# A hand-written order for the start of an attention + MoE kernel, and weights' lower parts without GpSimd

## The chip, the cores and the metric

The kernel runs on one core of a Trainium2 chip. The metric is the device time of one execution in microseconds (us). A core has five engines that matter here: TensorE (PE; PEld is its weight load) multiplies matrices, VectorE (DVE) and ScalarE (ACT) do elementwise work, GpSimd (POOL) does elementwise work and issues DMAs, and SyncE (SP) issues DMAs. Each engine takes its instructions in the order in which the compiler queued them. Matrix products go to PSUM; all other tiles lie in SBUF.

## The reference

```python
# q, k, v: [8, 8, 576, 64];  w_in: [512, 2048];  w_out: [2048, 512]; drawn inputs scale q by 8.0 and k by 4.405
q_s = softmax(q, axis=-1)              # over the 64 of a head
k_s = softmax(k, axis=2)               # over the 576 of the sequence
kv  = einsum('bhsd,bhse->bhde', k_s, v)
x   = einsum('bhsd,bhde->bhse', q_s, kv)      # then heads side by side: [4608, 512]
h   = x @ w_in
out = (h * clip(h + 3, 0, 6) / 6) @ w_out     # [4608, 512], float32
```

(The softmaxes add 1e-9 to their sums.)

## The kernel before, in words

The 4608 tokens are nine blocks of 512. The hidden width 2048 is 16 chunks `f` of 128. For a block `j` and a chunk `f`, `gemm1` makes 128 hidden rows (12 matmuls of 128x512 into a PSUM tile `ph`), applies the activation (ScalarE L567, VectorE L568) and splits the result `g` into an upper part `g_hi` (ScalarE, L123) and a lower part `g_lo` (VectorE, L124). `gemm2` adds that chunk's share to the four PSUM tiles `po` of the block (12 matmuls). Each product is made from upper and lower parts of both factors: hi*hi, hi*lo and lo*hi. Blocks 0 and 1 run in this form; blocks 2 to 8 take two chunks at a time by a scheme of seven products (`fast_pair`), whose combined weights block 1 works out (`fast_weights`) and stores to DRAM.

The weights arrive as raw 64-bit numbers, 1 MB a chunk (`load_w`, SyncE's queue). `decode(f)` turns them into 32-bit floats: ScalarE takes the magnitude (L145) and scales the low words (L156); VectorE clamps (L146), shifts (L148), merges the sign (L153) and adds the low words (L157); then `split` copies the upper part on ScalarE (L123) and subtracts on L124 for the lower part. That last subtraction is GpSimd's for odd chunks from 3 on, and VectorE's for the others. The tile `m` of a decode has one buffer, `v` two.

Attention of a block is done for four head pairs `hp`: the k softmax (VectorE km L262, ScalarE Exp L263, transposes on TensorE, copies L271 and L272), the q softmax (block 0: VectorE qm L252, GpSimd L253, ScalarE Exp L254, VectorE qr L255 to L257, GpSimd L258; transposes; copy L359), the product `pkv` with its normalisation into `kv` (VectorE L210 to L213), then `px` and its split into `x_hi` (ScalarE) and `x_lo` (VectorE). For block 0 the operands lie in the buffers of the weight chunks 15 to 8, which are loaded later. From block 2 on the softmax of q takes other lines (L292 to L302) and uses GpSimd for small copies (`swap` L284, `kb` L335).

What sets the order: the framework's scheduler simulates the program at compile time and orders each engine's instructions by readiness and by the order in which the program wrote them. `keep_in_program_order` fixes a TensorE instruction to the written order; the list `in_order` switches that on, and it is empty until block 1 begins. So in block 0 and ahead of it the scheduler is free on all engines; from block 1 on TensorE's order is the written one. The start is written as

```python
units = [attention(0, hp) for hp in range(NP)]
for unit in units:
    next(unit)
for unit in units:
    next(unit)
    next(unit)
decode(0)
for unit in units:
    next(unit, None)
decode(1)
```

and then, at each step (j, f) of blocks 0 and 1: `gemm1(j, f)`; in block 0 `decode(f + 2)`, in block 1 the combined weights; one step of the next block's attention (`step`); and `fill()`, which writes out all of the `gemm2` that is pending, the one of chunk f - 1.

Of the kernel before, what the change touches and what calls it, by code (L numbers as in the profile page):

```python
# [18 lines left out]
P = 128  # L19
TB = 512  # L20
# [10 lines left out]
def attention_moe(  # L31
# [57 lines left out]
    def mm(out, lhsT, rhs, start, stop, goes_on=False):  # L89
        ordered(  # L90
            nc.tensor.matmul(  # L91
                out, lhsT, rhs, start=start, stop=stop, skip_group_check=goes_on
            )
        )

    def flip(out, in_):
        ordered(nc.tensor.transpose(out, in_, ident))
# [33 lines left out]
            raws[f][:, a:b], w[f].rearrange("p s n -> p (s n)")[:, a:b]  # L131
        )

    def decode(f):

        n = 2 * DM
        pairs = raws.pop(f).rearrange("p (n two) -> p n two", two=2)
        low, high = pairs[:, :, 0], pairs[:, :, 1]
        m = moe.tile([P, n], F32, name="m", bufs=1)
        nc.scalar.activation(m, high.bitcast(F32), AF.Abs)  # L145
        nc.vector.tensor_scalar(m, m, W_MIN, W_MAX, op0=ALU.max, op1=ALU.min)  # L146
        m = m.bitcast(U32)
        nc.vector.tensor_scalar(  # L148
            m, m, 3, 0x3FFFFFFF, op0=ALU.logical_shift_left, op1=ALU.bitwise_and
        )  # L150
        v = moe.tile([P, n], F32, name="v", bufs=2)
        vu = v.bitcast(U32)
        nc.vector.scalar_tensor_tensor(  # L153
            vu, high, 0xC0000000, m, op0=ALU.bitwise_and, op1=ALU.bitwise_or
        )
        nc.scalar.activation(low, low, AF.Copy, scale=2.0**-29)  # L156
        nc.vector.tensor_tensor(vu, vu, low, op=ALU.add)  # L157
# [7 lines left out]
        wi[f], wo[f] = parts[:, 0], parts[:, 1]  # L165

    FAST = 2
    x_tiles = {}
# [32 lines left out]
    def kv_of(j, hp, ke, vt):  # L201

        pkv = ps_a.tile([P, TB], F32, name="pkv", tag="pa")
        for c in range(NCH):
            r = slice(0, P if c < NC4 else TAIL)
            for h in range(2):
                hs = slice(h * D, (h + 1) * D)
                mm(pkv[hs, 0 : D + 1], ke[r, c, hs], vt[r, c, h, :], c == 0, c == NCH - 1)
        rk = att.tile([P, 1], F32, name="rk", bufs=2)
        nc.vector.tensor_scalar_add(rk, pkv[:, D : D + 1], EPS)  # L210
        nc.vector.reciprocal(rk, rk)
        kv = att.tile([P, P], F32, name="kv", bufs=5)
        nc.vector.scalar_tensor_tensor(  # L213
            kv.rearrange("p (h d) -> p h d", h=2),
            pkv[:, 0:D].rearrange("p (o d) -> p o d", o=1).broadcast_to([P, 2, D]),
            rk,
            mask.rearrange("p (h d) -> p h d", h=2),
            op0=ALU.mult,
            op1=ALU.mult,
        )  # L220
        kvs[j, hp] = kv
# [14 lines left out]
    def q_softmax(qt, lean, pool):  # L236

        qs = qt.rearrange("p c h d -> p (c h) d")
        qm = att.tile([P, n8], F32, name="qm", bufs=2)
        qr = att.tile([P, n8], F32, name="qr", bufs=2)  # L240
        if lean:
            nc.vector.tensor_reduce(qm, qs, axis=AX.X, op=ALU.max, negate=True)
            for i in range(n8):
                nc.scalar.activation(
                    qs[:, i],
                    qs[:, i],
                    AF.Exp,
                    bias=qm[:, i : i + 1],
                    accum_out=qr[:, i : i + 1],
                )  # L250
        else:
            nc.vector.tensor_reduce(qm, qs, axis=AX.X, op=ALU.max)  # L252
            pool.tensor_sub(qs, qs, over(qm))  # L253
            nc.scalar.activation(qs, qs, AF.Exp)  # L254
            nc.vector.tensor_reduce(qr, qs, axis=AX.X, op=ALU.add)  # L255
        nc.vector.tensor_scalar_add(qr, qr, EPS)
        nc.vector.reciprocal(qr, qr)  # L257
        pool.tensor_mul(qs, qs, over(qr))  # L258

    def k_softmax(j, km, ke, kt):  # L260

        nc.vector.tensor_reduce(km, kt, axis=AX.X, op=ALU.max, negate=True)  # L262
        nc.scalar.activation(kt, kt, AF.Exp, bias=km)  # L263
        yield
        pool, tag = (ps_a, "pa") if j else (ps_o, "po")
# [5 lines left out]
        nc.scalar.copy(ke[:, 0:NC4].rearrange("p c n -> p (c n)"), pe)  # L271
        nc.scalar.copy(ke[0:TAIL, NC4], pe2[0:TAIL, 0:P])  # L272

    NG = TB // QD

# [29 lines left out]
    def attention(j, hp):  # L305
# [2 lines left out]


        early = j < 2  # L310
        if not j:
            kt, qt, qT, vt, ke = first[hp]
        else:
            if j < B:
                kt = att.tile([P, S], F32, name="kt", bufs=1)
                nc.sync.dma_start(kt, kT[j, hp])
                ke = att.tile([P, NCH, P], F32, name="ke", bufs=2)
                if not early:
                    nc.sync.dma_start(ke, k[j, hp].rearrange("p c h d -> p c (h d)"))
                vt = att.tile([P, NCH, 2, D + 1], F32, name="vt", bufs=2)  # L320
                nc.sync.dma_start(vt, v[j, hp])
            qt = att.tile([P, TB], F32, name="qt", bufs=2)
            nc.sync.dma_start(qt, q[j, hp] if early else qf[j - 2, hp])
            if early:
                qt = qt.rearrange("p (c h d) -> p c h d", c=NC4, h=2)

        if j < B:
            km = att.tile([P, 1], F32, name="km", bufs=2)
            if early:
                ks = k_softmax(j, km, ke, kt)  # L330
                next(ks)
            else:
                nc.vector.tensor_reduce(km, kt, axis=AX.X, op=ALU.max)
                kb = att.tile([P, P], F32, name="kb", bufs=1)
                nc.gpsimd.tensor_copy(kb, km.broadcast_to([P, P]))  # L335
        if early:
            q_softmax(qt, j == 1, nc.vector if j else nc.gpsimd)
        else:
            qT = q_softmax_t(qt)
        yield  # L340

        if early:
            next(ks, None)
        elif j < B:

            pm = ps_a.tile([P, TB], F32, name="pm", tag="pa")
            flip(pm[:, 0:P], kb)
            nc.vector.tensor_sub(
                ke, ke, pm[:, 0:P].rearrange("p (o n) -> p o n", o=1).broadcast_to([P, NCH, P])
            )  # L350
            nc.scalar.activation(ke, ke, AF.Exp)
        if early:
            pool, tag = (ps_a, "pa") if j else (ps_o, "po")
            tp = pool.tile([P, TB], F32, name="tp", tag=tag)
            for c in range(NC4):
                flip(tp[:, c * P : (c + 1) * P], qt[:, c].rearrange("p h d -> p (h d)"))
            if j:
                qT = att.tile([P, TB], F32, name="qT", tag="qT_hi")
            nc.scalar.copy(qT, tp)  # L359
        else:  # L360
            qT_hi = att.tile([P, TB], F32R, name="qT_hi")
            qT_lo = att.tile([P, TB], F32R, name="qT_lo")
            split(qT_hi, qT_lo, qT)
        yield

        if j < B:
            kv_of(j, hp, ke, vt)
            if not early:
                kv_split(j, hp)
            yield  # L370


        pool, tag = (ps_a, "pa") if j else (ps_h, "ph")
        px = pool.tile([P, TB], F32, name="px", tag=tag)
        e = SHIFT * j
        for b, lo, hi in ((j - 1, 0, e), (j, e, TB)):
            if lo < hi:
# [241 lines left out]
    for unit in units:  # L619
        next(unit)  # L620
    for unit in units:
        next(unit)
        next(unit)
    decode(0)
    for unit in units:
        next(unit, None)
    decode(1)

# [31 lines left out]
    def fill(n=10**6):  # L660
        while pend and n:
# [4 lines left out]
            got[0](*got[1])  # L666
            n -= 1

    for j in range(FAST):
        for f in range(NFC):  # L670
            if j == 0:
# [15 lines left out]
            pend.append(work(j, [f], [g]))  # L687
    for j in range(FAST, NB):
        for pair in range(NFC // 2):
# [73 lines left out]
```

## Time and profile before

| | |
|---|---|
| Median of 3 runs | 896.59 us (896.31 to 898.5) |
| The profiled execution | 896.98 us, of which the span of its instructions is 895.2 |
| TensorE busy | 863.4 us, 96% of the span |
| VectorE busy | 625.9 us, 70% |
| ScalarE busy | 458.7 us, 51% |
| GpSimd busy | 148.8 us, 17% |
| DMA | 182.05 MB, mean 203 GB/s |

Times of the profile count from the start of the span. A row of a timeline gives start, duration, engine, line, operation, the tile written and the tiles read, the shape and the count; in brackets stands how long the engine was idle before it, and what it waited for. A row of a group gives, behind the count, total busy time and mean duration in ns (or, in the view of one tile, the smallest, the median and the largest), then idle time before. Durations of neighbours on one engine overlap by some hundredths of a us, since the next instruction enters before the last has left. A row of a wait gives total, times and the longest. L123 and L124 are the lines of `split`, L91 the one of all matmuls, so the tile names tell what is meant.

### The profile page before, as it was taken

To read this page: it belongs to the slowest core of one execution; us is meant where nothing else is said; L and a number is where in the kernel's file an instruction comes from. 1 tells how busy PE (TensorE), PEld (TensorE's weight loads), DVE (VectorE), ACT (ScalarE), POOL (GpSimd) and SP (SyncE) were. 2 spreads that over 40 slices of the span, in tenths; PEclk is the share of its full clock that TensorE was granted. 3 is DMA by queue.
4 is the path that set the end of the run, shared out by engine and by line. 5 is a ranking of instruction groups with operands and counts; after the bars stand their busy time and mean duration, and the time that the engine had idled before them with its cause. 6 is when DMAs were issued, how large, how long until landed. Compare 5 with 4: busy or idle time off the path is not lost.

```text
span 895.2 us, 15285 instructions
## 1 busy us (share of the span) xinstructions
PE 863.4 (96%) x5380; PEld 739.4 (83%) x5380; DVE 625.9 (70%) x1265; ACT 458.7 (51%) x938; POOL 148.8 (17%) x330
## 2 busy tenths in 40 slices
PE   4799998999989999999999999999999999999998
PEld 3577766877878888888888888888888888989896
DVE  7999997889867666666777676767676655444333
ACT  7897653444445455454554554445554544443333
POOL 5112142221203121211121211112121210100000
PEclk9799999999999999999999999999999999999999
DMA  9982342439477677766776667666755575557541
GB/s 370 415 338 88 99 155 84 149 107 306 163 228 248 218 219 239 222 218 212 223 243 217 208 223 251 209 220 197 242 170 166 163 219 173 173 175 230 168 141 47
DMA packets 96843, 182.05 MB, mean 203 GB/s; under 512 B 9728, under 2 KB 24064, under 8 KB 94720
## 3 DMA queue, kind: packets, MB, share of 16 engines
q1 hardware_dynamic: 96192, 180.03, 61.8%
q8 instruction: 43, 0.70, 0.3%
q10 hardware_dynamic: 576, 1.05, 0.3%
q14 instruction: 32, 0.26, 0.1%
HBM read 156.93 MB, written 24.12 MB: 202 GB/s over the span
## 4 chain that ended last, share of the span: by engine, by line
PE 74%; DVE 6%; DMA 3%; ACT 2%; issue 1%; POOL 0%; DVEq 0%; ACTq 0%; POOLq 0%
PE po L91 36%; PE ph L91 29%; PE pz L91 4%; PE px L91 2%; PE pkv L91 2%; DMA qt<-in_qf_dram 2%; DMA out_dram<-ob 1%; DVE qT_lo L124 1%; DVE m L302 1%; DVE x_hi L124 1%; DVE g_lo L124 1%; DVE x_lo L124 0%; DVE g L568 0%; POOL swap L284 0%; DVE ob L599 0%
## 5 line engine op out<-in xcount | busy, mean ns | idle before, releaser
L91 PE MATMUL po<-w,w 128*128 128x512 f32 x1008 | 260.9, 394 | 1.0 <-DVE ob L599 1.0
L91 PEld LDWEIGHTS po<-w,w 128*128 128x128 f32 x1008 | 177.9, 188 | 31.4 <-DVE ob L599 2.1
L91 PE MATMUL ph<-x_lo,w 128*128 128x256 f32 (+1 forms) x800 | 151.9, 304 | 0.8 <-ACT second L529 0.8
L91 PEld LDWEIGHTS ph<-w,w 128*128 128x128 f32 x1008 | 134.2, 190 | 14.0 <-DVE second L530 4.9
L91 PE MATMUL ph<-w,w 128*128 128x256 f32 x1008 | 141.5, 285 | 2.9 <-DVE second L530 2.9
L91 PE MATMUL ph<-x_hi,w 128*128 128x256 f32 (+1 forms) x592 | 137.7, 336 | 2.4 <-DVE w L124 1.8
L91 PEld LDWEIGHTS ph<-x_lo,w 128*128 128x128 f32 x800 | 116.8, 189 | 15.5 <-ACT second L529 1.2
L123 ACT CAST w<-g 128x512 fp32r<-128x512 f32 x112 | 69.5, 620 | 88.0 <-DVE g L536 44.6
L91 PEld LDWEIGHTS ph<-x_hi,w 128*128 128x128 f32 x592 | 92.7, 190 | 16.2 <-DVE w L124 3.1
L124 DVE TENSOR_TENSOR w<-g,w 128x512 fp32r<-128x512 f32 x112 | 77.2, 689 | 39.1 <-ACT w L123 39.0
L91 PE MATMUL po<-w 128*128 128x512 f32 x336 | 86.8, 394 | 0.1
L91 PE MATMUL po<-w,g_hi 128*128 128x512 f32 x256 | 69.1, 407 | 2.0 <-ACT g_hi L123 1.7
L124 DVE TENSOR_TENSOR qT_lo<-m,qT_hi 128x512 fp32r<-128x512 f32 x28 | 24.1, 859 | 64.6 <-ACT qT_hi L123 64.6
L91 PEld LDWEIGHTS po<-w 128*128 128x128 f32 x336 | 59.4, 188 | 10.8 <-ACT w L123 0.5
L284 POOL COPY swap<-qm 32x16 f32<-32x16 f32 x112 | 36.1, 322 | 144.7 <-DVE qm L292 125.9
L91 PEld LDWEIGHTS po<-w,g_hi 128*128 128x128 f32 x256 | 47.4, 191 | 14.0 <-ACT g_hi L123 3.6
L551 ACT ACTIVATE g<-second,three 128x512 f32<-128x512 f32 x56 | 40.5, 723 | 30.1 <-DVE second L549 27.3
L535 ACT ACTIVATE g<-ph,three 128x256 f32<-128x256 f32 x56 | 26.5, 473 | 55.4 <-PE ph L91 55.1
L552 DVE SCALAR_TENSOR_TENSOR g<-g,second 128x512 f32<-128x512 f32 x56 | 39.0, 696 | 20.1 <-ACT g L551 20.1
L91 PE MATMUL pz<-x_hi,w 128*128 128x256 f32 x336 | 49.5, 283 | 0.0
L530 DVE TENSOR_TENSOR second<-second,ph 128x256 f32<-128x256 f32 x56 | 22.9, 410 | 37.0 <-ACT second L529 36.9
L536 DVE SCALAR_TENSOR_TENSOR g<-g,ph 128x256 f32<-128x256 f32 x56 | 23.2, 414 | 31.7 <-ACT g L535 31.7
(123 smaller groups left out, 1276.9 us busy)
## 6 DMA issues: line engine op xcount, KB each, us to landing
w<-wf SPq DMA_DIRECT2D x392, 256.0 KB, 3.1
raw<-in_w_dram SPq DMA_DIRECT2D x16, 1024.0 KB, 13.4
out_dram<-ob SPq DMA_DIRECT2D x36, 256.0 KB, 3.2
vt<-in_v_dram SPq DMA_DIRECT2D x28, 325.0 KB, 3.5
wf<-w SPq DMA_DIRECT2D x16, 512.0 KB, 4.6
kt<-in_kT_dram SPq DMA_DIRECT2D x28, 288.0 KB, 2.9
ke<-in_k_dram SPq DMA_DIRECT2D x24, 320.0 KB, 2.9
qt<-in_qf_dram SPq DMA_DIRECT2D x28, 256.0 KB, 3.2
```

The lines of the kernel that those rows point to most:

```text
L91: nc.tensor.matmul(out, lhsT, rhs, start=start, stop=stop, skip_group_check=goes_on)
L123: nc.scalar.copy(hi, src)
L124: engine.tensor_sub(lo, src, hi.bitcast(F32))
L284: nc.gpsimd.tensor_copy(swap[r : r + QD], stat[o : o + QD])
L302: nc.vector.transpose(qT, qt)
L530: nc.vector.tensor_add(second[:, HT:], second[:, HT:], y)
L535: nc.scalar.activation(r[:, HT:], x, AF.Relu, bias=three, scale=1.0)
L536: nc.vector.scalar_tensor_tensor(r[:, HT:], r[:, HT:], 6.0, x, op0=ALU.min, op1=ALU.mult)
L551: nc.scalar.activation(r, second, AF.Relu, bias=three, scale=1.0)
L552: nc.vector.scalar_tensor_tensor(r, r, 6.0, second, op0=ALU.min, op1=ALU.mult)
```

## The change

Five things are changed.

1. Ahead of the loops, the calls above are replaced by a list, `HEAD`. Block 0's attention is cut into steps of three kinds for each head pair (`k`, `q`, `x`), and `decode` into eight steps (`decode_steps`, which also issues L156's scaling right behind L145's magnitude). The list names them in order, with the decodes of chunks 0, 1 and 2 woven in. While it is written out, all instructions of VectorE and ScalarE in it are pinned to the written order (`Pinned`), and TensorE's too.
2. Whatever the loop writes on VectorE and ScalarE at its first step, and at its second up to the step of attention, is ordered behind the last pinned instruction of its engine (`behind`).
3. Lower parts of weights: chunks below 10 are subtracted on VectorE. From chunk 10 on ScalarE writes the negative of `v`, rounded, and a DMA issued from GpSimd's queue adds `v` to it in place.
4. In block 0 `decode` runs three chunks ahead of `gemm1` instead of two.
5. In block 0 one pending `gemm2` is kept back, so that the `gemm2` of chunk f - 2 stands behind `gemm1` of chunk f. In block 1 all pending ones are written out, as before.

```diff
-    in_order = []
+    in_order = [True]
...
+    class Pinned:
...
+                ins = getattr(self.engine, op)(*args, **kwargs)
+                if by_hand:
+                    tc.keep_in_program_order(ins)
+                    last[self.engine.engine] = ins
+                return ins
...
+    by_hand, last = [True], {}
+    dve, act = Pinned(nc.vector), Pinned(nc.scalar)
...
+    BY_DMA = 10
...
-    def decode(f):
+    def decode_steps(f):
...
-        nc.scalar.activation(m, high.bitcast(F32), AF.Abs)
-        nc.vector.tensor_scalar(m, m, W_MIN, W_MAX, op0=ALU.max, op1=ALU.min)
+        act.activation(m, high.bitcast(F32), AF.Abs)
+        yield
+        act.activation(low, low, AF.Copy, scale=2.0**-29)
+        yield
+        dve.tensor_scalar(m, m, W_MIN, W_MAX, op0=ALU.max, op1=ALU.min)
+        yield
...
-        nc.scalar.activation(low, low, AF.Copy, scale=2.0**-29)
-        nc.vector.tensor_tensor(vu, vu, low, op=ALU.add)
+        yield
+        dve.tensor_tensor(vu, vu, low, op=ALU.add)
+        yield
...
-        split(
-            parts[:, :, 0],
-            parts[:, :, 1],
-            v.rearrange("p (s n) -> p s n", s=2),
-            nc.gpsimd if f % 2 and f > 1 else nc.vector,
-        )
+        vs = v.rearrange("p (s n) -> p s n", s=2)
+        if f < BY_DMA:
+            act.copy(parts[:, :, 0], vs)
+            yield
+            dve.tensor_sub(parts[:, :, 1], vs, parts[:, :, 0].bitcast(F32))
+        else:
+            hi, lo = parts[:, :, 0], parts[:, :, 1]
+            act.copy(hi, vs)
+            act.mul(lo, vs, -1.0)
+            nc.gpsimd.dma_start(lo.bitcast(F32), vs, accum_op=ALU.add)
...
+    def first_k(hp):     # 6 steps: km | Exp | transposes | copies | pkv | rk, kv
+    def first_q(hp):     # 5 steps: qm, GpSimd sub | Exp | qr, GpSimd mul | transposes | copy
+    def first_x(hp):     # 3 steps: px | x_hi | x_lo
...
-    units = [attention(0, hp) for hp in range(NP)]
...
-    decode(1)
+    HEAD = """
+        k0 q0 k0 k1 k0 q1 k1 q0 k0 k1 q1 q0 k1 q1 w0 w0 q0 q0 q1
+        q2 k2 w0 k0 k2 q2 q1 q3 k3 k2 w0 q2 k3 q3 k2 k1 k3 q3 k3
+        w0 k0 k1 k2 q2 x0 q2 w0 k2 w1 x0 w0 k3 q3 w1 w1 x0 k3 q3 x1 x1
+        w1 w0 x2 x1 x2 w1 x2 x3 x3 w2 w1 w2 x3 w2 w1 w2 w1 w2 w2 w2 w2
+    """
...
+    for name in HEAD.split():
+        next(parts_of[name], None)
...
+    in_order.clear()
+    by_hand.clear()
+    behind = ExitStack()
+    for ins in last.values():
+        behind.enter_context(tc.issue_after(ins.ins))
...
             if j == 0:
-                if f + 2 < NFC:
-                    decode(f + 2)
+                if f + 3 < NFC:
+                    decode(f + 3)
...
+            if (j, f) == (0, 1):
+                behind.close()
             next(step, None)
-            fill()
+
+            while len(pend) > 1 - j:
+                fill_one()
             pend.append(work(j, [f], [g]))
```

`fill_one` writes out the oldest pending `gemm2` whole. The comments behind `first_k`, `first_q` and `first_x` stand for their bodies, which issue the same instructions as `attention` did for block 0.

More of the change, by code (lines that the diff above doesn't have):

```diff
@@ L94, in mm, with __init__, __getattr__, issue @@
         )
+    class Pinned:
+        def __init__(self, engine):
+            self.engine = engine
+        def __getattr__(self, op):
+            def issue(*args, **kwargs):
+                ins = getattr(self.engine, op)(*args, **kwargs)
[3 more added lines that the diff above has]
+                return ins
+            return issue
+    by_hand, last = [True], {}
+    dve, act = Pinned(nc.vector), Pinned(nc.scalar)
     def flip(out, in_):
@@ L270, in k_softmax, with q_flip @@
         flip(pe2[0:TAIL, 0:P], kt[:, TB:S])
-        nc.scalar.copy(ke[:, 0:NC4].rearrange("p c n -> p (c n)"), pe)
-        nc.scalar.copy(ke[0:TAIL, NC4], pe2[0:TAIL, 0:P])
+        yield
+        act.copy(ke[:, 0:NC4].rearrange("p c n -> p (c n)"), pe)
+        act.copy(ke[0:TAIL, NC4], pe2[0:TAIL, 0:P])
+    def q_flip(pool, tag, qt, qT):
+        tp = pool.tile([P, TB], F32, name="tp", tag=tag)
+        for c in range(NC4):
+            flip(tp[:, c * P : (c + 1) * P], qt[:, c].rearrange("p h d -> p (h d)"))
+        yield
+        act.copy(qT, tp)
+    def first_k(hp):
+        kt, _, _, vt, ke = first[hp]
+        km = att.tile([P, 1], F32, name="km", bufs=2)
+        yield from k_softmax(ps_o, "po", km, ke, kt)
+        yield
+        yield from kv_of(0, hp, ke, vt)
+    def first_q(hp):
+        _, qt, qT, _, _ = first[hp]
+        yield from q_softmax(qt, False, nc.gpsimd)
+        yield
+        yield from q_flip(ps_o, "po", qt, qT)
+    def first_x(hp):
+        qT = first[hp][2]
+        pool, tag = (ps_h, "ph") if hp < 2 else (ps_a, "pa")
+        px = pool.tile([P, TB], F32, name="px", tag=tag)
+        mm(px, kvs[0, hp], qT, True, True)
+        yield
+        x_hi, x_lo = (t[:, hp, :] for t in x_block(0))
+        act.copy(x_hi, px)
+        yield
+        dve.tensor_sub(x_lo, px, x_hi.bitcast(F32))
+    STEPS0 = {"k": first_k, "q": first_q, "x": first_x}
     NG = TB // QD
@@ L310, in attention @@
         early = j < 2
[L311 to L325, printed above, removed]
+        if j < B:
+            kt = att.tile([P, S], F32, name="kt", bufs=1)
+            nc.sync.dma_start(kt, kT[j, hp])
+            ke = att.tile([P, NCH, P], F32, name="ke", bufs=2)
+            if not early:
+                nc.sync.dma_start(ke, k[j, hp].rearrange("p c h d -> p c (h d)"))
+            vt = att.tile([P, NCH, 2, D + 1], F32, name="vt", bufs=2)
+            nc.sync.dma_start(vt, v[j, hp])
+        qt = att.tile([P, TB], F32, name="qt", bufs=2)
+        nc.sync.dma_start(qt, q[j, hp] if early else qf[j - 2, hp])
+        if early:
+            qt = qt.rearrange("p (c h d) -> p c h d", c=NC4, h=2)
         if j < B:
@@ L329, in attention @@
             if early:
-                ks = k_softmax(j, km, ke, kt)
-                next(ks)
+                ks = k_softmax(ps_a, "pa", km, ke, kt)
+                for _ in range(2):
+                    next(ks)
             else:
@@ L336, in attention @@
         if early:
-            q_softmax(qt, j == 1, nc.vector if j else nc.gpsimd)
+            for _ in q_softmax(qt, True, nc.vector):
+                pass
         else:
@@ L342, in attention @@
         if early:
-            next(ks, None)
+            for _ in ks:
+                pass
         elif j < B:
@@ L352, in attention @@
         if early:
[L353 to L359, printed above, removed]
+            qT = att.tile([P, TB], F32, name="qT", tag="qT_hi")
+            for _ in q_flip(ps_a, "pa", qt, qT):
+                pass
         else:
@@ L366, in attention @@
         if j < B:
-            kv_of(j, hp, ke, vt)
+            for _ in kv_of(j, hp, ke, vt):
+                pass
             if not early:
@@ L667, in fill, with fill_one @@
             n -= 1
+    def fill_one():
+        for fn, x in pend.pop(0):
+            fn(*x)
     for j in range(FAST):
```

55 lines of the change are left out of this document (29 added, 26 removed).

## Prediction

> **What bounds the kernel now.** I began with the span and a table of busy time by stretch. Its columns are length, busy time and instructions of each engine, granted clock and DMA share.
>
> ```profile
> span 895.2 us, 15285 instructions
> ```
>
> ```profile
> 0.00:34.00 34.00, 17.78 (x124) 12.64 (x125) 28.36 (x51) 26.75 (x39) 11.31 (x19) 0.87 0.96 384
> 34.00:152.25 118.25, 112.22 (x531) 85.22 (x529) 113.89 (x165) 80.91 (x164) 29.37 (x32) 0.96 0.49 177
> 152.25:250.00 97.75, 96.73 (x510) 77.32 (x509) 82.38 (x179) 44.77 (x85) 20.69 (x53) 1.00 0.55 180
> 250.00:895.00 645.00, 636.69 (x4221) 564.23 (x4219) 401.32 (x871) 306.27 (x654) 87.47 (x226) 1.00 0.64 202
> ```
>
> After 152 us TensorE (first busy column) is busy 99% of the time and works in a written order: whatever is won before that point is carried to the end whole, and nothing after it is touched. The first two stretches are VectorE's (third column). From 34 to 152 us, block 0, it is busy 113.89 of 118.25 us. The change edits only these two stretches, so I read them next: VectorE's instructions in order of time beside GpSimd's, then grouped by line over 34 to 152 us.
>
> ```profile
> 40.02 2.40 POOL L124 TENSOR_TENSOR w<-v,w 128x1024 fp32r<-128x1024 f32 x1 [18.27 <-ACT w L123]
> ...
> 71.03 3.50 POOL L124 TENSOR_TENSOR w<-v,w 128x1024 fp32r<-128x1024 f32 x1 [11.32 <-ACT w L123]
> ```
>
> ```profile
> 40.03 2.94 DVE L148 TENSOR_SCALAR m<-m 128x1024 uint32<-128x1024 uint32 x1
> ...
> 49.31 0.69 DVE L148 TENSOR_SCALAR m<-m 128x1024 uint32<-128x1024 uint32 x1
> ```
>
> ```profile
> L153 DVE SCALAR_TENSOR_TENSOR v<-raw,m 128x1024 uint32<-128x1024 uint32 x13 | 20.1, 1543 | 0.3
> L157 DVE CUSTOM_DVE_ANT_0 v<-raw,v 128x2048 uint16<-128x2048 uint16 x13 | 15.8, 1215 | 0.0
> L124 DVE TENSOR_TENSOR g_lo<-g,g_hi 128x512 fp32r<-128x512 f32 x17 | 15.2, 895 | 0.0
> L148 DVE TENSOR_SCALAR m<-m 128x1024 uint32<-128x1024 uint32 x13 | 14.1, 1081 | 0.2
> L568 DVE SCALAR_TENSOR_TENSOR g<-g,ph 128x512 f32<-128x512 f32 x17 | 11.5, 678 | 1.1 <-ACT g L567 1.1
> L124 DVE TENSOR_TENSOR w<-v,w 128x1024 fp32r<-128x1024 f32 x7 | 8.4, 1204 | 0.0
> L146 DVE TENSOR_SCALAR m<-m 128x1024 f32<-128x1024 f32 x12 | 8.2, 683 | 0.0
> ```
>
> A subtraction on GpSimd takes 2.40 us, and the VectorE instruction that meets it stretches with it: L148 takes 2.94 us at 40.03, and 0.69 at 49.31 with GpSimd idle. So GpSimd's seven subtractions are paid for on the engine that bounds the stage. The group means show the same: each of L153, L148 and the g_lo subtraction stands above its clean neighbour of like size (L157 1215 ns, L146 683, L568 678).
>
> **Term 1, the weights' lower parts.** The stretch that goes is 13 x (1543 - 1215) + 13 x (1081 - 683) + 17 x (895 - 678) ns = 4.3 + 5.2 + 3.7 = 13.1 us of VectorE time, about 1.9 for each GpSimd subtraction. Chunks 3, 5, 7 and 9 come to VectorE: 4 x 1.204 = 4.8 us more. Chunks 10, 12 and 14 leave it: 3 x 1.204 = 3.6 us less. Net 13.1 - 4.8 + 3.6 = **11.9 us less VectorE work**.
>
> The six chunks from 10 on get a ScalarE multiplication and a DMA that accumulates.
>
> ```profile
> L123 ACT CAST w<-v 128x1024 fp32r<-128x1024 f32 x10 | 10.5, 1053 | 3.6 <-DVE v L157 3.0 <-DVE rk L210 0.6
> ```
>
> Six multiplications at this row's 1.05 us are 6.3 us on ScalarE, which is busy 80.91 of 118.25: 87 us of work in a stage of some 110 still fits, so zero is taken; without that idle time it would cost all 6.3. The accumulating DMA has no like in this trace: GpSimd issues none. The nearest transfers:
>
> ```profile
> wf<-w SPq DMA_DIRECT2D x1, 512.0 KB, 2.9
> ```
>
> ```profile
> raw<-in_w_dram SPq DMA_DIRECT2D x16, 1024.0 KB, 13.4
> ```
>
> It moves 512 KB within the chip's fast memory at a time when the DMA engines are half idle (share 0.49), so I take 2.9 us to landing, with 13.4 (twice the bytes under full load) as the other end. Against VectorE's 1.2 us subtraction, that makes chunk 10's low part about 2.8 us later, multiplication included. The cover is one second GEMM, 2.79 us by the chain's row below, which the longer lag keeps in hand; without it the 2.8 is paid once, since from chunk 10 on VectorE has 1.2 us less per even chunk. Whether issuing it blocks VectorE is not shown. The ends are nothing and the 1.9 us of a subtraction, six times (11.4 us, which would leave a loss). I take nothing, because no operand passes through GpSimd. The issue waits on ScalarE and holds GpSimd's queue; behind it stand only block 2's swap and kb copies, wanted after 250 us. The SP queue's stores of weights wait for the DMA in block 1, long after.
>
> **Term 2, the written order.** Here the trace before is good: VectorE starts at 4.50 and then hardly waits.
>
> ```profile
> 4.50 0.75 DVE L262 TENSOR_REDUCE km<-kq 128x1 f32<-128x576 f32 x1 [4.50 <-DMA kq<-in_kT_dram]
> ...
> 35.19 1.22 DVE L153 SCALAR_TENSOR_TENSOR v<-raw,m 128x1024 uint32<-128x1024 uint32 x1
> 36.33 0.74 DVE L262 TENSOR_REDUCE km<-kt 128x1 f32<-128x576 f32 x1
> 36.99 0.68 DVE L124 TENSOR_TENSOR x_lo<-px,x_hi 128x512 fp32r<-128x512 f32 x1
> 37.59 1.21 DVE L157 CUSTOM_DVE_ANT_0 v<-raw,v 128x2048 uint16<-128x2048 uint16 x1
> 38.72 0.68 DVE L242 TENSOR_REDUCE qm<-qt 128x8 f32<-128x512 f32 x1
> 39.31 0.68 DVE L146 TENSOR_SCALAR m<-m 128x1024 f32<-128x1024 f32 x1
> ```
>
> The new order gives VectorE 9 instructions for each of four head pairs and 5 for each of three chunks, 51 in all, as many as the first stretch holds now in 28.36 us. Without a wait it would be through at 4.5 + 28.9 = 33.4 us (two short clamps and shifts less, a subtraction and an x_lo more). But VectorE may no longer pass over an instruction that isn't ready.
>
> ```profile
> L253 POOL TENSOR_TENSOR kq<-kq,qm x4: 1035/1042/1490, 5.9 to 13.8; 128x512 f32<-128x512 f32 x4
> L254 ACT ACTIVATE kq<-kq x4: 614/631/633, 7.3 to 14.9; 128x512 f32<-128x512 f32 x4
> ```
>
> I walked the list with the durations of these rows and of the group rows, each instruction starting at the later of its engine's turn and its input. The list leaves VectorE waiting for the first q's GpSimd and Exp (1.0 us), the last q's Exp (0.5), chunk 1's Abs (1.0), px of pair 1 on a slow TensorE (1.0), chunk 2's Abs (0.4), and the copies of chunks 1 and 2 (0.8 and 1.1). That is 5.8 us, or about 3.6 with TensorE at full clock, so it ends between 37 and 39; I take **38.0**.
>
> Before, VectorE stands at 39.31 with all that done, and chunk 3's four operations (1.22, 1.21 and two of 0.68) and block 1's first two reductions (0.74 and 0.68), 5.2 us, on top. The same state is reached at 38.0 + 5.2 = 43.2: **3.9 us lost**. The ends: no waits, 0.7 won; the waits doubled (11.6), 10.9 lost. Everything behind the last pinned instruction queues there: chunk 0's L567 and L568, and with them the PSUM buffer for the third GEMM. TensorE idles before that GEMM for a us or two near 38; it waits in the same place now:
>
> ```profile
> 43.62 0.50 PE L91 MATMUL ph<-x_hi,w 128*128 128x512 f32 x1 [0.63 <-DVE g L568]
> ```
>
> The walk has the last px at 29 to 31 us and its x_lo done by 31.5, against 36.99 + 0.68 = 37.67. The first GEMM can so begin near 31.
>
> **Term 3, the lag.**
>
> ```profile
> 34.02 1.41 PE L91 MATMUL ph<-x_hi,w 128*128 128x512 f32 x1
> ...
> 152.02 0.39 PE L91 MATMUL po<-w,g_lo 128*128 128x512 f32 x1
> ```
>
> ```profile
> PE ph L91 <- DVE w L124: 1.8, 3, 0.9
> PE po L91 <- ACT g_hi L123: 1.7, 1, 1.7
> PE po L91 <- DVE g_lo L124: 1.6, 2, 1.3
> ```
>
> ```profile
> 188.69 2.79 PE po L91 x12
> ```
>
> These are TensorE's named waits between its first block-0 GEMM and the last of block 0. A second chunk's GEMM in hand (2.79 us) covers the largest, 1.7 us for the last g_hi. But while VectorE sets the pace a covered wait turns into another one, so by itself I price the lag at nothing; were VectorE no longer the bound, these waits are the 5.1 us it could save.
>
> **Sum.** VectorE ends block 0 11.9 - 3.9 = 8.0 us earlier. TensorE can follow: 3 us of earlier start and 5.1 us of waits make 8.1. From the profiled execution's 896.98: 889.0. The runs' median lies 0.4 lower, so **888.6**.
>
> **Rivals.**
>
> *A: the written order eats the gain.* The first stretch runs without a gap now, which speaks for it; the earlier x_lo speaks against. With the waits doubled the sum is 11.9 - 10.9 = 1.0 us won, 895.6.
>
> *B, slower: the accumulating DMAs land late.* Chunks 10 to 15 need their low part in the third matmul of each group. At the 13.4 us end, less the 2.8 of one GEMM in hand, TensorE stands still 10.6 us, once, as the six overlap: 888.6 + 10.6 = 899.2. It decides from about 11 us to landing. For it: no such DMA in the trace, and GpSimd's own work was held up by VectorE, 3.50 us at 71.03 against 2.40. Against it: the 2.9 us row and half-idle DMA engines. The Trainium skill ("SBUF — State Buffer", SBUF: two separate sides) says that a DMA issued from GpSimd can't get its descriptors written while VectorE runs an instruction in a two-port mode. That rule speaks against this change; the 3.50 us row agrees that GpSimd waits for VectorE, but no run here shows it for descriptors. The clean instructions that could block last 0.68 us, so the delay stays far under 11 us, and I keep B small.
>
> *C: TensorE becomes the bound, and more is won.* With no waits in the list the sum is 11.9 + 0.7 = 12.6 us, and block 0 would end on TensorE, whose granted clock (0.96 in the stage) could also rise: 884.0.
>
> *D: the freed time isn't used.* The compiler's own order behind the list fills VectorE with block 2's preparation, which already runs by 110 us, and the end of block 0 stays: 896.6.
>
> ```profile
> 110.29 0.67 DVE L292 TENSOR_REDUCE qm<-qt 128x16 f32<-128x512 f32 x1
> ```
>
> **Chances.** Forecast 0.62, C 0.14, A 0.10, D 0.05, B 0.09. What this measurement can tell from no change is 0.3%, 2.7 us. Faster are the forecast and C, and half of A: 0.81; the same the other half of A and D: 0.10; slower B: 0.09. The forecast's own range, with 37 to 39 and the smaller unknowns, is 885.5 to 891.5; for eight in ten it reaches to C's far side and to A: 882.0 to 895.5.
>
> **What would show it.** L153, L148 and g_lo at about 1.22, 0.69 and 0.68 us in block 0, with no GpSimd subtraction of weights (term 1). The first ph matmul near 31 us, and VectorE's last pinned subtraction ending at 37 to 39 (term 2). The last po of block 0 near 144 instead of 152, with no g_hi wait before it (term 3). The prediction is wrong if VectorE stays stretched while the six DMAs are issued, if low parts of chunks 10 to 15 appear as TensorE's releaser for more than 3 us, or if block 1 shows new waits that give the 8 us back.

## The result, and the profile after

The change made the kernel slower: 906.98 us median (905.75 to 909.14, 4 runs) beside 896.93 for the kernel before (896.31 to 898.5, 4 runs). The ratio is 1.0111, with a 95% interval of 1.0094 to 1.0128, so about 10 us where 8 us of gain were forecast. The profiled execution took 909.14 us. Its busy time by stretch, cut where the prediction cut (the last stretch runs to the new end):

```profile
0.00:34.00 34.00, 22.55 (x145) 14.61 (x146) 27.36 (x50) 23.54 (x36) 10.81 (x19) 1.00 0.97 384
34.00:152.25 118.25, 98.26 (x467) 75.02 (x466) 100.11 (x157) 85.58 (x166) 15.04 (x27) 0.93 0.64 198
152.25:250.00 97.75, 96.45 (x487) 77.23 (x486) 79.55 (x168) 44.19 (x83) 19.96 (x48) 1.00 0.53 174
250.00:907.00 657.00, 648.17 (x4286) 573.55 (x4284) 409.13 (x892) 310.91 (x661) 89.19 (x236) 0.99 0.64 200
```

TensorE did more in the first stretch (22.55 us against 17.78) and 14 us less in the second (98.26 against 112.22). VectorE, busy 113.89 us of that stretch before, is now busy 100.11 and no longer bounds it. Part of that drop is work that comes later now (block 0 ends at 162.2 us, behind the stretch); over the whole run VectorE is busy 9.8 us less (616.1 against 625.9), where 11.9 were forecast. Block 2's first matmul, at 247.2 us before, comes at 257.1, so 9.9 us are lost by then. The two profiled executions end 12.2 us apart (spans of 907.4 and 895.2), the medians 10; the 2.3 us that this trace loses behind 257.1, with a granted clock of 0.99 there against 1.00, lie within the spread of the kernel's own runs (905.75 to 909.14).

TensorE's named waits in the new trace, from 25 to 260 us (total, times, longest):

```profile
PE ph L92 <- DMA w<-v: 12.2, 4, 8.2
PE ph L92 <- DVE g L638: 4.0, 1, 4.0
PE po L92 <- ACT g_hi L143: 2.5, 3, 1.8
PE ph L92 <- DVE x_lo L105: 1.5, 2, 0.8
PE ph L92 <- ACT w L105: 0.9, 1, 0.9
```

The first line is new: the accumulating DMA that makes the lower part of a weight chunk holds up `gemm1` four times, once for 8.2 us. Around that longest wait the timeline reads (start, duration; in brackets the idle time before it, and its releaser):

```profile
105.76 1.28 POOL L358 COPY swap<-qr 32x16 f32<-32x16 f32 x4
...
109.91 1.06 ACT L105 ACTIVATE w<-v 128x1024 fp32r<-128x1024 f32 x1
...
112.56 0.75 DVE L405 TENSOR_REDUCE km<-kt 128x1 f32<-128x576 f32 x1 [3.49 <-DMA kt<-in_kT_dram]
...
113.44 0.62 POOL L407 COPY kb<-km 128x128 f32<-128x128 f32 x1 [6.40 <-DVE km L405]
114.06 1.22 POOL L197 DMA_DIRECT2D w<-v  x1
...
118.60 1.05 ACT L105 ACTIVATE w<-v 128x1024 fp32r<-128x1024 f32 x1
...
121.79 0.50 PEld L92 LDWEIGHTS ph<-x_hi,w 128*128 128x128 f32 x2 [8.68 <-DMA w<-v]
121.80 1.22 PE L92 MATMUL ph<-x_hi,w 128*128 128x512 f32 x2 [8.25 <-DMA w<-v]
121.80 0.38 SPq L521 DMA_DIRECT2D wf<-w  x1
121.84 1.22 DVE L105 SCALAR_TENSOR_TENSOR v<-raw,m 128x1024 uint32<-128x1024 uint32 x1 [0.21 <-DMA w<-v]
122.01 1.20 POOL L197 DMA_DIRECT2D w<-v  x1 [3.70 <-ACT qt L369]
122.27 0.42 SPq L387 DMA_DIRECT2D kt<-in_kT_dram  x1
...
125.66 0.75 DVE L405 TENSOR_REDUCE km<-kt 128x1 f32<-128x576 f32 x1 [2.38 <-DMA kt<-in_kT_dram]
```

This is chunk 11. ScalarE's negative was ready at 110.97 (109.91 + 1.06). GpSimd stood idle, but its queue's next instruction was block 2's copy L407, which waited 6.40 us for VectorE's L405, which waited for a load of `kt` (issued at 107.06, on the chain for 5.47 us). The issue of the accumulating DMA stood behind that copy and left at 114.06, 3.1 us after its input was there; it took 1.22 us of GpSimd, and the data landed 7.7 us after the issue began. TensorE waited 8.25 us. VectorE's next decode waited 0.21 us for the same landing: `v` has two buffers, and the DMA reads one of them until it lands.

Two more things hang on the landing. Chunk 12's issue came late with no copy ahead of it: its negative was ready at 119.65 (118.60 + 1.05), GpSimd stood idle for 3.70 us, and the issue left at 122.01, 0.2 us after chunk 11 had landed (114.06 + 7.7). In none of the four traces with these DMAs (this one, e2, e5 and e12 below) does an issue leave before the one ahead of it has landed. What makes it wait is not shown: here the profile names ScalarE's L369, which ended at 121.69, and in e5 and e12 others. And SyncE's stores of weights to DRAM (`wf`, L521), which wait for the same lower parts, run in block 0 already, with loads for block 2 behind them in the queue: one store left at 121.80, as chunk 11 landed, the load of `kt` behind it at 122.27, and at 125.66 VectorE had waited 2.38 us for that load. SyncE's waits from 85 to 160 us begin with

```profile
SPq L521 <- DMA w<-v: 33.2, 6, 8.2
```

TensorE came back at a lower granted clock (the last column but two of these 10 us stretches):

```profile
110.00:120.00 10.00, 3.55 (x16) 2.32 (x15) 7.44 (x14) 5.14 (x7) 3.52 (x6) 0.84 0.85 224
120.00:130.00 10.00, 8.20 (x24) 6.33 (x25) 7.21 (x13) 3.44 (x7) 1.96 (x5) 0.65 0.63 148
```

The DMAs issued between 60 and 150 us (size, median us to landing):

```profile
w<-v POOLq DMA_DIRECT2D x6, 512.0 KB, 5.5
```

The prediction took 2.9. VectorE's own waits from 34 to 152 us, which had no line with a load before, begin with one:

```profile
DVE km L405 <- DMA kt<-in_kT_dram: 5.9, 2, 3.5
```

The start of the kernel did move forward. Its first `ph` matmul, the last pinned instruction of VectorE and the third GEMM:

```profile
23.97 0.79 PE L92 MATMUL ph<-x_hi,w 128*128 128x512 f32 x1
...
35.94 1.23 DVE L105 TENSOR_TENSOR w<-v,w 128x1024 fp32r<-128x1024 f32 x1 [1.17 <-ACT w L105]
...
39.07 0.79 PE L92 MATMUL ph<-x_hi,w 128*128 128x512 f32 x1 [4.04 <-DVE g L638]
```

The first GEMM begins 10 us earlier than before and the third 4.5 us earlier (39.07 against 43.62). By chunk 4's GEMM the lead is gone (61.0 against 56.8). Chunk 11's begins at 112.8 against 101.7, and chunk 12's, behind the long wait, at 126.3 against 112.0.

### The profile page after: what moved, and what is told of

Same layout as the page of the kernel before. It is cut to its first block, busy times and chain, and to the rows that moved or that the text cites. A ratio compares the mean times of both kernels' runs of the same rounds, so it can differ in the third digit from the quotient of the medians.

```text
span 907.4 us, 15313 instructions
## 1 busy us (share of the span) xinstructions
PE 865.4 (95%) x5380; PEld 740.4 (82%) x5380; DVE 616.1 (68%) x1266; ACT 464.2 (51%) x944; POOL 135.0 (15%) x329
## 3 DMA queue, kind: packets, MB, share of 16 engines
q10 hardware_dynamic: 576, 1.05, 0.3%
## 4 chain that ended last, share of the span: by engine, by line
PE 79%; DVE 7%; DMA 6%; ACT 6%; issue 2%; POOL 0%; SPq 0%; ACTq 0%; POOLq 0%; DVEq 0%
PE po L92 37%; PE ph L92 31%; PE pz L92 4%; PE pkv L92 3%; PE px L92 2%; DMA w<-v 2%; ACT raw L105 1%; DMA qt<-in_qf_dram 1%; ACT w L105 1%; DVE v L105 1%; DMA out_dram<-ob 1%; ACT m L105 1%; DVE qT_lo L144 1%; DMA kt<-in_kT_dram 1%; ACT qt L105 1%
## 5 line engine op out<-in xcount | busy, mean ns | idle before, releaser
L92 PE MATMUL ph<-x_hi,w 128*128 128x256 f32 (+1 forms) x592 | 140.4, 342 | 18.2 <-DMA w<-v 12.2
```

Source lines behind the costliest of these rows:

```text
L92: nc.tensor.matmul(out, lhsT, rhs, start=start, stop=stop, skip_group_check=goes_on)
```

## The experiments

Every run below is compared with the kernel before on its own chip; the ratios are used, and 0.1% is 0.9 us. The kernel after was compared on another chip than the experiments, and these on five chips (e1 to e5, e6 to e9, e10 to e13, e14 to e16, e17 to e19), so a difference between two groups carries the intervals of both. The theories:

- **D**: the accumulating DMAs lose the time, by standing late in GpSimd's queue and landing late.
- **W**: the written order loses it (pinning, or the sequence itself).
- **L**: the longer lag or the third chunk of lead loses it.

| run | what is left of the change | median us | ratio to before (95%) |
|---|---|---|---|
| e4 | lower parts all on VectorE, nothing else | 895.15 | 0.9959 (0.9943 to 0.9975) |
| e5 | e4's start, DMAs from chunk 10 | 901.70 | 1.0033 (1.0020 to 1.0046) |
| e1 | all of it but the DMAs | 900.52 | 1.0017 (1.0003 to 1.0030) |
| e6 | e1 without the lag | 899.15 | 1.0016 (1.0002 to 1.0029) |
| after | all of it | 906.98 | 1.0111 (1.0094 to 1.0128) |

### Part by part

No DMA (e1), and the DMAs in front of block 2's copies (e2):

```diff
 e1
-    BY_DMA = 10
+    BY_DMA = 16
 e2
-            nc.gpsimd.dma_start(lo.bitcast(F32), vs, accum_op=ALU.add)
+            sums.append(nc.gpsimd.dma_start(lo.bitcast(F32), vs, accum_op=ALU.add))
...
+        if j == 1:
+            behind_sums.enter_context(tc.issue_after(sums[-1].ins))
...
+    behind_sums.close()
```

> The changed kernel with all 16 lower parts subtracted on VectorE, so no accumulating DMA; the rest of the change stays. If the six DMAs are what turned a gain into a loss (by whatever mechanism), TensorE's 12.2 us of waits for them go and the time falls below the kernel before: 885 to 891. VectorE's sum gives 13.1 us of stretch won, 7 more subtractions of 1.2 us paid, 3.9 us of head lost at most. If the written order or the lag costs the time, it stays at 900 or above.

> The changed kernel, with GpSimd's copies for block 2 (swap and kb) ordered behind the six accumulating DMAs on GpSimd's queue; nothing else is edited. Queue theory: the issue for chunk 11 stood behind a kb copy that waited for a load of kt, so the 8.2 us wait of TensorE goes, and with it the slow clock behind it: 890 to 897. Landing theory: each DMA takes 5 to 8 us and holds one of two v buffers until it lands, so decode(f+2) waits for it whatever the queue does: TensorE still waits 8 us or more in total for the DMAs and the time stays at 900 to 907.

e1: 1.0017, so 0.94% (8.4 us) of the loss goes with the DMAs. e2: 902.66 us, 1.0045 (1.0030 to 1.0061): with block 2's GpSimd copies queued behind the last accumulating DMA, 0.66% (5.9 us) comes back. TensorE's wait for the DMAs is down from 12.2 to 5.1 us while the landing is not faster; e2's rows of waits and of DMAs:

```profile
PE ph L92 <- DMA w<-v: 5.1, 3, 3.3
```

```profile
w<-v POOLq DMA_DIRECT2D x6, 512.0 KB, 5.8
```

So most of the DMAs' cost goes when block 2's copies stand behind them; the landing stays at 5.8 us. How much of it is the place in the queue alone isn't shown, since the edit does more: VectorE's work that needs those copies moves too. From 90 to 139 us VectorE spends 9.0 us on block 2's attention in the kernel after and 2.9 in e2, and moving block 2's attention behind the decodes wins 0.23% with no DMA at all (e13 against e9, below).

The kernel before with GpSimd's subtractions on VectorE (e4), and with the new lower parts in the old order (e5):

```diff
 e4
-            nc.gpsimd if f % 2 and f > 1 else nc.vector,
+            nc.vector,
 e5: for f < 10 as e4, from chunk 10 on
+            nc.scalar.mul(lo, vs, -1.0)
+            nc.gpsimd.dma_start(lo.bitcast(F32), vs, accum_op=ALU.add)
```

> The kernel before, with only GpSimd's seven subtractions given to VectorE. By the stretch of VectorE's instructions (13.1 us) less seven subtractions of 1.2 us, VectorE ends block 0 some 4.7 us earlier: 891 to 893. If the stretch is no real cost of the stage, no change or slower: 896 to 900.

> The kernel before, with the lower parts made as in the changed kernel (chunks below 10 on VectorE, the others by ScalarE and an accumulating DMA), and nothing else of the change: no written order, lookahead of two chunks, lag of one. Landing theory: less lookahead makes it worse, TensorE waits for each of the six DMAs: 905 to 920. Queue theory: here only a swap copy or a kb copy stands between two issues, so it depends on those: 892 to 905. If the DMAs are harmless by themselves and the combination with the written order does the harm, 886 to 892.

e4: 0.9959, 3.7 us won by taking the seven subtractions off GpSimd alone. e5: 1.0033; against e4 the DMAs lose 0.74% (6.6 us) in the old order too. So the DMAs lose time with and without the written order. Here no copy holds an issue back: five of the six leave 0.3 to 0.4 us after their negative is ready, the sixth after 1.35, and that one 0.3 us after the landing ahead of it. So a place late in GpSimd's queue is not needed for the loss: what is left is the landing and what waits for it. From 34 to 152 us VectorE waits 9.2 us for loads of `qt` (5.0) and `kt` (4.2), where e4 has 0.2; no run separates that from TensorE's own waits. The six ScalarE multiplications come and go with the DMAs in all these runs; ScalarE is busy 31.0 of the 57 us from 95 to 152 in the kernel after, and 29.0 of the 50 from 95 to 145 in e5, so it is not full there. e5's waits of TensorE and its landing:

```profile
PE ph L91 <- DMA w<-v: 5.6, 4, 1.5
PE po L91 <- ACT g_hi L123: 4.7, 4, 2.3
```

```profile
w<-v POOLq DMA_DIRECT2D x6, 512.0 KB, 6.4
```

The lag alone, undone in e1's kernel (e6) and done in e4's (e7):

```diff
 e6
-            while len(pend) > 1 - j:
-                fill_one()
+            fill()
 e7
-            fill()
+            while len(pend) > 1 - j:
+                for fn, x in pend.pop(0):
+                    fn(*x)
```

> e1 (the written order, all lower parts on VectorE) with the GEMM lag undone: all pending second GEMMs are written out at each step, as before. e1 stands some 5 us above the kernel before with the same edit (e4). If the lag is what costs them: 893 to 897, at e4's 895. If the written order (head) does: 899 to 902, as e1. If the lag is a gain inside e1: 902 to 906.

> e4 (the kernel before with all lower parts on VectorE) with the longer lag and nothing else: one second GEMM is kept back in block 0; decode stays two chunks ahead. Lag costs: 899 to 902. Head costs: 894 to 896, as e4, or a us or two less, as TensorE's waits for g_hi (3.0 us in e4) are covered.

e6: 1.0016, as e1. e7: 896.58 us, 0.9985 (0.9972 to 0.9998), 0.26% above e4. The lag brings nothing and costs between nothing and 2.3 us. What is left between e4 and e6 is the written order with its lead of three chunks: 0.57% (5.1 us).

### What in the written order costs it

The first guesses were about single steps of the head. The scaling of the low words (L156's operation) may stand far ahead of its use on ScalarE; e8 orders it behind the same chunk's magnitude in e1's kernel, e9 in e4's. e10 takes chunk 2 out of the list (`decode(2)` is called behind it) and drops the ordering behind it, e11 drops that ordering alone; both start from e6.

```diff
 e8, e9
-        nc.scalar.activation(low, low, AF.Copy, scale=2.0**-29)
+        with tc.issue_after(first_of.ins):       # the magnitude of this chunk
+            nc.scalar.activation(low, low, AF.Copy, scale=2.0**-29)
 e10, e11
-    for ins in last.values():
-        behind.enter_context(tc.issue_after(ins.ins))
 e10, in HEAD
-        w1 w0 x2 x1 x2 w1 x2 x3 x3 w2 w1 w2 x3 w2 w1 w2 w1 w2 w2 w2 w2
+        w1 w0 x2 x1 x2 w1 x2 x3 x3 w1 x3 w1 w1
```

> e1 with each chunk's scaling of the low words queued on ScalarE behind the magnitude (Abs) of the same chunk, so that it can't be pulled ahead; no instruction is added or removed. ScalarE theory: in e1 ScalarE is 100% busy from 40 to 60 us, three scalings of far chunks (3.2 us) stand in a row ahead of an Abs and of a g_hi for which TensorE waits 2.41 us, and TensorE does only 7.35 us of work in 50 to 60. Without them 4 to 6 us come back: 894 to 897. If VectorE's own work behind the list is the limit there, no change: 899 to 902.

> e4 with the same ordering of the low words' scaling, in the order of the kernel before. ScalarE theory: ScalarE is full from 40 to 70 us here too (10.0, 10.0 and 9.9 of 10 us), but TensorE is not starved there (10.0 of 10), so little is won: 892 to 896. If the scalings pulled ahead are useful later (ScalarE has less to do after 70 us), it gets slower: 896 to 899.

> e6 (the written order, lower parts on VectorE, short lag) with chunk 2's decode taken out of the list and left to the scheduler, and nothing ordered behind the list any more. List theory: the list's tail holds only chunk 2, so VectorE and ScalarE wait for each other there (1.2 and 4.1 us in e8's trace), and chunk 3 and block 1's first reductions start only after it; that is the 4 us between e6 (899) and e4 (895). Then 894 to 896. If the order of block 0's attention itself costs the time, 898 to 901.

> e6 with only the ordering behind the list taken away: the list stays, but the first steps of the loop may slip in ahead of its last instructions. If that ordering is what makes chunk 3 late: 894 to 897. If the list as such is: 898 to 901, as e6.

e8: 901.17 us, 1.0034 (1.0019 to 1.0048), no gain. e9: 892.05 us, 0.9932 (0.9914 to 0.9951), better than e4 by 0.27% in the old order, with intervals that overlap. e10: 899.06 us, 1.0012 (0.9999 to 1.0025); e11: 899.41 us, 1.0016 (1.0002 to 1.0030): neither chunk 2 in the list nor the ordering behind it is the cost.

That left pinning, the list's sequence as the scheduler sees it, and the lead. e14 is e10 with the old lead of two, e15 is e4 with a lead of three, e16 is e6 with its list written out but nothing pinned.

```diff
 e14, from e10
-    decode(2)
...
-                if f + 3 < NFC:
-                    decode(f + 3)
+                if f + 2 < NFC:
+                    decode(f + 2)
 e15, from e4: the opposite edit
 e16, from e6
-    in_order = [True]
+    in_order = []
-    by_hand, last = [True], {}
+    by_hand, last = [], {}
```

> The kernel after with all lower parts on VectorE, the lag undone, chunk 2 out of the list, nothing ordered behind it, and decode two chunks ahead of the first GEMM again. What is left of the change, beside the kernel before with all lower parts on VectorE (895.15 us), is the pinned list of block 0's attention and of chunks 0 and 1. Theory P, the pinned list costs the 4 us: 899, as with the lead of three (899.06). Theory L, the third chunk of lead costs them, since its decode takes VectorE and ScalarE from the activations of the first chunks: 895, and TensorE's idle time before the third GEMM goes from 4.0 us to under 1.5.

> The kernel before with all lower parts on VectorE and decode three chunks ahead of the first GEMM, chunk 2's decode written behind chunk 1's ahead of the loops; nothing pinned, the attention in its order of before. Theory L (the third chunk of lead costs 4 us): 899. Theory P (the pinned list costs them): 895.

> All lower parts on VectorE, short lag, lead of three, the start written out in the list's order, but nothing pinned and nothing ordered behind it: the scheduler is free. If pinning costs the 4 us: 895, and VectorE passes over instructions that are not ready. If the written sequence or the lead of three costs them: 899.

e14: 898.12 us, 1.0007 (0.9993 to 1.0022), as e10 (1.0012). e15: 893.65 us, 0.9955 (0.9939 to 0.9972), as e4: the lead of three is innocent. e16: 893.03 us, 0.9948 (0.9929 to 0.9968): the same text without pins is 0.68% (6.1 us) faster than e6. The cost is pinning. Then one engine at a time, from e16's kernel:

```diff
 e17
-    by_hand, last = [], {}
-    dve, act = Pinned(nc.vector), Pinned(nc.scalar)
+    by_hand, last = [True], {}
+    dve, act = Pinned(nc.vector), nc.scalar
 e18: instead
+    dve, act = nc.vector, Pinned(nc.scalar)
```

Nothing is ordered behind the list in either, as in e16.

> As the run with the list not pinned (893.0 us), but with VectorE's instructions of the list in the written order; ScalarE and TensorE stay free. VectorE's busy time up to 80 us is 72.6 us without pins and 65.8 with all three engines pinned. If VectorE's own order is the cost: 899, with some 66 us of busy time. If it was held up by ScalarE's or TensorE's order: 893 to 895, with 71 us or more.

> The same with ScalarE's instructions of the list in the written order; VectorE and TensorE stay free. If ScalarE's order is the cost: 899, with VectorE busy for some 66 us up to 80 us, since its inputs come late. If not: 893 to 895.

e17: 891.79 us, 0.9918 (0.9890 to 0.9945): VectorE's written order costs nothing. e18: 896.07 us, 0.9982 (0.9968 to 0.9996), 0.34% (3.0 us) above e16: ScalarE's order alone costs about half of it. (These two intervals just touch; e17, on e18's chip, is 0.64% below e18, with intervals apart.) VectorE is busy for 72.2 us up to 80 us in e17 and 69.7 in e18, beside 72.6 in e16: the 66 that e18's theory named did not come. The other half needs TensorE's pins or several engines' together; no run pins TensorE alone, so that stays open. The stretch from 20 to 40 us of e16, e17, e18 and e6, in this order (VectorE is the third busy column, ScalarE the fourth):

```profile
20.00:40.00 20.00, 15.93 (x74) 9.93 (x73) 19.86 (x30) 18.37 (x24) 1.86 (x1) 0.94 1.02 413
```

```profile
20.00:40.00 20.00, 17.26 (x92) 11.33 (x93) 19.40 (x30) 18.65 (x37) 0.00 (x0) 0.91 1.02 415
```

```profile
20.00:40.00 20.00, 14.99 (x65) 8.96 (x64) 17.00 (x24) 18.11 (x29) 0.57 (x1) 0.91 1.02 416
```

```profile
20.00:40.00 20.00, 13.27 (x62) 7.52 (x61) 17.71 (x27) 16.50 (x20) 0.00 (x0) 0.96 1.02 415
```

VectorE is full (19.86, 19.40) when ScalarE is free, and loses 2 to 3 us when ScalarE is pinned, even where its own order is free (17.00). The kernel after shows two places, in ScalarE's timeline:

```profile
20.52 0.58 ACT L105 COPY kq<-tp 128x512 f32<-128x512 f32 x1 [1.79 <-PE tp L117]
21.00 1.14 ACT L105 ACTIVATE m<-raw 128x1024 f32<-128x1024 f32 x1
...
34.87 1.04 ACT L105 CAST w<-v 128x1024 fp32r<-128x1024 f32 x1 [2.03 <-DVE v L105]
35.82 0.68 ACT L637 ACTIVATE g<-ph,three 128x512 f32<-128x512 f32 x1
```

At 20.52 a pinned copy waits 1.79 us for TensorE's transposes, with chunk 1's magnitude behind it. At 34.87 a pinned copy waits for VectorE's chunk, and the first GEMM's activation stands behind it, as the change orders it. In e16 the same activation starts at 33.30 and its third GEMM at 34.98 instead of 39.07.

The second place is not the cost by itself: in e11, where nothing is ordered behind the list, the activation starts at 33.70, and e11 is as slow as e6. The first is there, with 1.8 to 4.1 us, in every run that pins ScalarE (2.8 in e18 and e11), and not in e16, e17 or e19. In e18 VectorE's largest wait, from 5 to 40 us, is

```profile
DVE rk L248 <- PE pkv L92: 2.5, 1, 2.5
```

No run moves that copy alone, so which of ScalarE's waits costs the time stays open.

### Block 2's preparation, and the best version

e12 puts block 2's attention behind chunk 15's decode on VectorE, ScalarE and GpSimd, in the kernel after; e13 does the same on VectorE and ScalarE in e9's; e19 takes e16's kernel with e9's and e13's edits.

```diff
 e12; e13 and e19 alike, with the last chunk's two instructions
-            next(step, None)
+            with ExitStack() as after_decode:
+                if j:
+                    for ins in (added[0], *ends[-2:]):
+                        after_decode.enter_context(tc.issue_after(ins.ins))
+                next(step, None)
```

> The changed kernel with block 2's attention queued, on VectorE, ScalarE and GpSimd, behind the last decode (chunk 15's addition, its ScalarE multiplication and its accumulating DMA). No instruction is added or removed. Queue theory for all engines: VectorE waits 5.9 us in the changed kernel for loads of kt that block 2's km needs, with decodes behind them, and GpSimd's issue for chunk 11 waits behind kb. Both go, and with them most of the DMAs' 6.5 us: 898 to 901. If landing and the v buffers are the rest, TensorE still waits some 5 us for the DMAs: 902 to 904.

> e9 (the order of the kernel before, lower parts on VectorE, low words behind Abs: 892) with block 2's attention queued behind chunk 15's last two decode instructions. Some 12 us of block 2's VectorE work, which runs from 110 to 150 us, leaves the stage that VectorE bounds: block 0 ends 3 to 8 us earlier, and blocks 1 and 2 have idle VectorE time for it: 885 to 890. If block 1 then waits for that work (its attention steps stand in TensorE's written order), the gain is given back: 890 to 894.

> What the runs point to, taken together: all lower parts on VectorE, the list's text with nothing pinned, lead of three, no lag, the scaling of the low words right behind the magnitude on ScalarE, and block 2's attention behind chunk 15's decode on VectorE and ScalarE. The last two gave 3.1 and 2.5 us in the order of before (895.15 to 892.05 to 889.56). If they add to the list's text (893.0): 887.5. If the list's text already has what the scaling's place gives (in the list the scaling stands right behind the magnitude): 890.5.

e12: 902.96 us, 1.0054 (1.0035 to 1.0074): like e2, it takes back 0.57%, and like e2 it leaves the landing. e13: 889.56 us, 0.9909 (0.9892 to 0.9925), 0.23% below e9 with intervals that overlap. e19: 888.76 us, 0.9893 (0.9868 to 0.9918), about 1.1% faster than the kernel before. e13 and e19 can't be told apart by their intervals; both beat both kernels.

## Why the prediction was wrong

By ratios, going from before to after in four steps: GpSimd's subtractions to VectorE -0.41% (e4), the pinned list with its lead +0.57% (e6), the lag +0.01% (e1), the DMAs +0.94% (after), together +1.11%. In us: -3.7, +5.1, +0.1 and +8.4, where the prediction had -4.7 (its 13.1 less 7 x 1.204), +3.9, 0 and -7.2 (6 x 1.204). Of the 18 us between forecast and result, 15.6 lie in the last step.

**Term 1, the stretch: right.** The three groups that were to come down, in the kernel after:

```profile
L105 DVE SCALAR_TENSOR_TENSOR v<-raw,m 128x1024 uint32<-128x1024 uint32 x13 | 15.8, 1218 | 0.4 <-DMA w<-v 0.2
L144 DVE TENSOR_TENSOR g_lo<-g,g_hi 128x512 fp32r<-128x512 f32 x15 | 10.2, 678 | 0.2
L105 DVE TENSOR_SCALAR m<-m 128x1024 f32<-128x1024 f32 (+1 forms) x26 | 17.8, 686 | 2.3 <-ACT m L105 2.2
```

The last row holds the clamps and the shifts together. 1218, 678 and 686 ns stand where 1.22, 0.68 and 0.69 us were forecast. By itself this gave 3.7 of the 4.7 us (e4).

**Term 1, the accumulating DMA: the step that failed.** The prediction took the DMA as free: 2.9 us to landing, a delay that one GEMM covers, and nothing of weight behind it. Three parts of that failed.

The landing was mis-sized, 5.5 us instead of 2.9. The row chosen was a store of the same size from SyncE's queue, with no accumulation, and a single one: the sixteen stores of 512 KB in the trace before have a median of 4.6. The issues did not overlap either, so a late one made the next one late. The 2.79 us of one GEMM did not cover the sum: TensorE waited four times, 12.2 us. Without the longer lag 2.8 us were to be "paid once"; e5 has no longer lag, and there too TensorE waited four times, 5.6 us.

The issue, it wrote, "holds GpSimd's queue; behind it stand only block 2's swap and kb copies". It asked what stands behind the issue, not what can stand ahead of it. In the kernel after the scheduler put a copy ahead that waits for VectorE and a load, and chunk 11's issue waited with it, 3.1 us; e2, with the copies behind, took 5.9 us back.

"The SP queue's stores of weights wait for the DMA in block 1, long after": they waited in block 0, 33.2 us in all (in e1, without the DMAs, 21.1 us for VectorE's lower parts), with loads for block 2 behind them.

Where it expected VectorE's freed time to become TensorE's, VectorE was left idle for 18.14 us of the stage (118.25 less 100.11, by the table of stretches); the largest of its named waits is for block 2's loads, 5.9 us. How the 8.4 us divide between landing, queue and loads stays open: e5 loses 6.6 with no copy ahead of an issue, and e2 wins back 5.9 by an edit that also moves VectorE's work.

**Rival B** named the right part and sign, but not the mechanism or the size: it decided only from 11 us to landing, and the longest was 7.7. Its "once, as the six overlap" did not hold: none overlapped, and TensorE waited in four places. The Trainium skill's rule on descriptors, quoted there, isn't shown at work: each of the six issues took 1.20 to 1.34 us on GpSimd, and no run separates the descriptors from the transfer. The Trainium skill ("DMA: Bandwidth & Descriptors", Anatomy of one DMA — SWDGE (gpsimd) path) gives 2.0 us and the bytes at 436 KB a us for a DMA from this queue, 3.2 us for 512 KB as an estimate from that page; the six measured here, which accumulate, took 5.5.

**Rivals A and D** each had a part in it: the written order cost 5.1 us, where A put its cost at 10.9, and block 2's preparation in the middle of block 0, which is D's reason, costs some 2 us (e13 against e9, 0.23% with intervals that overlap).

**Term 2: near in size, wrong in place.** The list ended at 37.2 (35.94 + 1.23) where 37 to 39 was forecast, and cost 5.1 us where 3.9 was. The nearness of the cost is in part luck: the prediction charged it to VectorE, which may no longer pass over an instruction, and VectorE's order alone costs nothing (e17), while ScalarE's alone costs 3.0 (e18). The first GEMM, forecast near 31, came at 23.97, and this early start bought nothing: the third GEMM then waited 4.0 us for `g`.

**Term 3: priced at nothing, and it is nothing or a small loss** (0.1 us from e6 to e1, 2.3 from e4 to e7).

**"Whatever is won before 152 us is carried to the end whole"** held for the loss, within the spread of the runs: 9.9 us at block 2's start, 12.2 at the end of the same two traces, 10 in the medians.

The prediction's own sign of failure, low parts of chunks 10 to 15 as TensorE's releaser for more than 3 us, is what the first row of waits shows, with 12.2. The last `po` of block 0, forecast near 144, ended at 162.2.

## What to carry to other kernels

When work is moved to a DMA queue that an engine also computes on, look at what the scheduler may put ahead of the issue, as well as at what waits behind it: an instruction there that waits for another engine or a load delays the DMA by what is left of its wait (here 3.1 of 6.40 us). Ask too what waits for the landing, in other queues as well: here stores, with the next block's loads behind them. Take a transfer's time from all rows of its size, not from one. In this kernel pinning the order of the full engine (VectorE) cost nothing, and pinning one that feeds it (ScalarE) cost 3.0 us; a pinned instruction that waits for its input holds up what is ready behind it. When several edits come together, run each alone: here one gained 3.7 us, and two others lost 13.5.

## What the runs showed that was not expected

A DMA that accumulates 512 KB within the fast memory, issued from GpSimd, lands in 5.5 to 6.4 us (medians of the kernel after, e2, e5 and e12) and takes 1.2 us of GpSimd for the issue, and the next one did not leave before it had landed. A subtraction of the same tile on VectorE takes 1.2 us. The DMA saves that time on VectorE and gains nothing where TensorE's next GEMM waits for the result.

After TensorE's wait of 8.25 us at chunk 11 the granted clock was 0.65 over the stretch from 120 to 130 us, and 1.00 over the next ten. A pair of 128x512 matmuls took 1.06 us there (at 123.24), and 0.63 ahead of the wait (at 110.61); behind the wait of 4.04 us at 39.07 it took 1.06 too. In this trace such a wait costs more than its own length; how long it must be for that, no run shows.
